# Transposing two heads at once, and putting the transposes behind the scores

## The chip, the cores and the metric

The kernel runs on one core of one Trainium2 chip. The metric is device time in microseconds of one execution, as the median over several. Times of single instructions come from one profiled execution, whose time differs a little from the median; both are given below.

## The reference

Eight batches, eight heads, 576 positions, head size 64. Causal attention with a decay bias, and behind it an MLP mixer: a token part (a product over positions) and a channel part (512 to 1536 to 512).

```python
scores = scale * np.matmul(q, k.transpose(0, 1, 3, 2))
s_pos = np.maximum(s, 0.0)
cum = np.cumsum(s_pos, axis=-1)
bias = -(cum[:, :, :, None] - cum[:, :, None, :])
scores = np.where(causal, -1000000000.0, scores + np.minimum(bias, 0.0))
attn = softmax(scores)
x = np.matmul(attn, v)                       # heads side by side: (8, 576, 512)
xt = x.transpose(0, 2, 1)
h = np.maximum(xt @ w_tok1, 0.0) @ w_tok2
u = x + h.transpose(0, 2, 1)
return u + np.maximum(u @ w_ch1, 0.0) @ w_ch2
```

(`softmax` stands for the subtraction of the maximum, the exponential and the division that the reference writes out.)

## The kernel before

All work is recorded as operations with the engines that may run them, an estimated duration on each, a priority and the tiles that they read and write. A planner (`Plan.run`) then goes through time, gives each free engine the ready operation of best priority, and hands out buffers from rings; the order that it finds is what is issued. TensorE (PE) runs matrix products, ScalarE (ACT) and VectorE (DVE) evict its results from PSUM and do the pointwise work, GpSimd (POOL) and the sync engine (SP) issue transfers. The planner's estimate of a change between 64-row and 128-row work on TensorE is the constant `SWITCH`; an operation with `mode=1` is 64-row work. A dependency given as `after` lets the second operation start as soon as the first has been issued.

Two rings lie in PSUM: `psc`, two buffers of two banks each (1024 float32), and `pmx`, four buffers of one bank. The channel part's products (L1039 for the first matrix, L1064 for the second), the token part's (L921, L983) and a few others use `pmx`; scores (L750) and the weighted sum of v (L821) use `psc`.

The work around the change goes by quads of four heads, two quads to a batch:

- `stage_qk` loads k and q of a quad in bfloat16 (L479). A tile `qkn` holds, for k and for q, two groups f of 9 x 64 numbers on each partition: partitions 0 to 63 are heads with e = 0, partitions 64 to 127 those with e = 1, and the nine blocks of 64 are positions p*9 + r. L664 takes sums of squares of `qkn` for a final check of ranges.
- `quad` transposes k (ti = 0) and then q (ti = 1). For each r, e and f one 64x64 transpose (L706) goes into PSUM, 36 for k and 36 for q. The data are the weights of the product and a 64x64 identity moves. Batch one writes into two `pmx` buffers, every later batch into the two banks of one `psc` buffer. Then ACT (L718) or DVE (L720) copies each half into `kT` or `qT`, in the right order of positions.
- `pair` takes two heads (f = 0 and 1 of one e), which lie in the two 64-row halves of the array. The scores stand in two pieces, each with a `psc` buffer and an operation of its own on TensorE: four products in the first and six in the second (L750). ACT takes the exponential (L758), DVE applies the causal mask (L767, L775), TensorE multiplies by v (L821, 18 products), and DVE divides (L850, L854).

The first quad of batch one comes by another way: it is loaded in float32 and cast by L541 and L543 into the same layout.

After attention, `tok` and `chan` do the mixer of a batch, whose products fill TensorE while the attention of the next batch goes on. Early gaps of TensorE are filled with products of zeros (L1160).

Of the kernel before, what the change touches and what calls it, by code (L numbers as in the profile page):

```python
# [9 lines left out]
BF16 = mybir.dt.bfloat16  # L10
# [22 lines left out]
class Buf:  # L33
# [14 lines left out]
    @property  # L48
    def t(self):
        return self.ring.tiles[self.slot]  # L50
# [187 lines left out]
def c_pe(n, f32=False):  # L238
    occ = n * (4 if f32 else 1) / 2400.0 + 0.0025
    return occ, occ + 0.21  # L240


def c_act(n, bias=False):
    occ = 0.08 + n * 0.00088 + (0.093 if bias else 0.0)
    return occ, occ + 0.1


def c_dve(n, two=False):
    occ = 0.1 + n * (0.00056 if two else 0.00104)
    return occ, occ + 0.12  # L250
# [121 lines left out]
def kernel(  # L372
# [12 lines left out]
    nc = tc.nc  # L385

    B, H, S, D = q.shape
# [7 lines left out]
    NQ = 512  # L395
    LAG = 2.5
    WARM = 45.0
    TOK = 2.0
    R = 9
    PR = S // R  # L400
# [9 lines left out]
    def ring(name, n, shape, dt, pool=None):  # L410
        p = pool or fast
        return Ring(name, [p.tile(shape, dt, name=f"{name}{i}", tag=f"{name}{i}") for i in range(n)])

    ident = sb("ident", [128, 128], BF16)
# [15 lines left out]
        return EB[jc] + (64 if odd else 128) if jc == NJ - 2 else EB[jc] - (64 if odd else 0)  # L430

    r_qn = ring("qkn", 5, [128, 2, 2, R * D], BF16)
    r_qT = ring("qT", 4, [128, S], BF16)
    r_kT = ring("kT", 4, [128, 640], BF16)
    r_E = ring("E", 4, [128, 2, EW], BF16)
# [13 lines left out]
    r_sc = ring("psc", 2, [128, 1024], FP32, psum)  # L449
    r_mx = ring("pmx", 4, [128, 512], FP32, psum)  # L450

    P = Plan()
# [52 lines left out]
    for i in range(2, 4):  # L505
        P.op({"DVE": (0.3, 0.5, lambda i=i: pads(nc.vector, i)), "POOL": (0.4, 0.6, lambda i=i: pads(nc.gpsimd, i))},
             writes=[("pad", i)], prio=40)
    P.op({"DVE": (0.6, 0.8, lambda: pads2(nc.vector)), "POOL": (1.0, 1.2, lambda: pads2(nc.gpsimd))},
         writes=["padw"], prio=41)
    P.op({"DVE": (0.3, 0.5, lambda: pads3(nc.vector, 1)), "POOL": (0.5, 0.7, lambda: pads3(nc.gpsimd, 1))},  # L510
         writes=["padv"], prio=42)
# [18 lines left out]
    first = Buf(r_qn)  # L530
    stage = r_gb.tiles[0][:, :, :].rearrange("p c n -> p (c n)").bitcast(FP32)
    stage = stage[:, 0 : 4 * R * D].rearrange("p (t f n) -> p t f n", t=2, f=2)
    for ti, src in enumerate((k, q)):
        def load0(ti=ti, src=src):
            nc.sync.dma_start(out=stage[:, ti, :, :],
                              in_=src[0, 0:4, :, :].rearrange("(f e) (p r) d -> (e p) f (r d)", e=2, r=R))
        P.op({"SP": (0.6, 4.0 + 0.9 * ti, load0)}, writes=[("stage", ti)], prio=-9 + ti)
        for f in range(2):
            def cast0(eng, ti=ti, f=f):
                if eng:  # L540
                    nc.vector.tensor_copy(out=first.t[:, ti, f, :], in_=stage[:, ti, f, :])  # L541
                else:
                    nc.scalar.copy(out=first.t[:, ti, f, :], in_=stage[:, ti, f, :])  # L543
            P.op({"ACT": (*c_act(576), lambda cast0=cast0: cast0(0)),
                  "DVE": (0.1 + 576 * 0.00104, 0.25 + 576 * 0.00104, lambda cast0=cast0: cast0(1))},
                 reads=[("stage", ti)], writes=[(first, ti, f)], prio=-6)
    P.op({"SP": (0.6, 4.8, lambda: nc.sync.dma_start(out=s_sb[:, :], in_=s.rearrange("b h s -> (b h) s")))},
         writes=["s"], prio=-7)
# [137 lines left out]
    xbuf = {}  # L686
    bd = Buf(r_mx, False)

    def quad(b, h):
        nat = qkn[(b, h)]  # L690
        np_ = (b * H + h) / 2
        dsts = [(Buf(r_kT), Buf(r_qT)) for e in range(2)]
        pads = [("pad", 2), ("pad", 3)] if b == 0 and h == 4 else []
        for ti in range(2):
            pts = [Buf(r_mx, False) for e in range(2)] if b == 0 else [Buf(r_sc, False)] * 2

            def pv(e, pts=pts):
                o = pts[e].t[:, :].bitcast(BF16)
                return o[:, 0:1024] if b == 0 else o[:, e * 1024 : e * 1024 + 1024]

            def tr(ti=ti, pv=pv):
                for r in range(R):
                    for e in range(2):
                        p0 = e * PR
                        for f in range(2):
                            nc.tensor.transpose(out=pv(e)[f * D : f * D + D, r * PR : (r + 1) * PR],  # L706
                                                in_=nat.t[p0 : p0 + PR, ti, f, r * D : (r + 1) * D],
                                                identity=ident[p0 : p0 + PR, p0 : p0 + PR])
            turn = P.op({"PE": (R * 0.031, R * 0.031 + 0.21, tr)}, reads=([(nat, ti, 0), (nat, ti, 1)] if b == 0 and h == 0 else [(nat, ti)]) + ["ident"] + pads,
                 writes=[(pts[e], e) for e in range(2)] + (["turned"] if b == 0 and h == 0 and ti == 0 else []), holds=[d[ti] for d in dsts], prio=(np_ - 30 * (b < 1 and h < 1), 2), mode=1)  # L710
            if b == 0 and h == 0 and ti == 1:
                scan.deps.add(turn)
            for e in range(2):
                def ev(eng, ti=ti, e=e, pv=pv):
                    i = pv(e)[:, 0:S].rearrange("d (r p) -> d p r", r=R)
                    o = dsts[e][ti].t[:, 0:S].rearrange("d (p r) -> d p r", r=R)
                    if eng == 0:
                        nc.scalar.copy(out=o, in_=i)  # L718
                    else:
                        nc.vector.tensor_copy(out=o, in_=i)  # L720
                P.op({"ACT": (*c_act(576), lambda ev=ev: ev(0)), "DVE": (*c_dve(576), lambda ev=ev: ev(1))},
                     reads=[(pts[e], e)], writes=[(dsts[e][ti], 0)], prio=1, alone=pts[e])
        for e in range(2):
            pair(b, h + e, *dsts[e])

    def pair(b, h, kT, qT):
        np_ = (b * H + h // 4 * 4) / 2 + h % 2
        E = Buf(r_E)
        odd = b % 2
        for pc, piece in enumerate(PIECES):  # L730
            ps = Buf(r_sc, False)
            c0 = 0
            cols = []
            for (jc, a, e) in piece:
                cols.append((jc, a, e, c0))
                c0 += e - a

            if b == 0:
                def preset(ps=ps, pc=pc):
                    for hh in range(2):  # L740
                        nc.tensor.matmul(out=ps.t[:, hh * 512 : hh * 512 + 512], lhsT=ident[:, :], rhs=neg[:, pc, :],  # L741
                                         start=True, stop=False)
                P.op({"PE": (2 * c_pe(512)[0], 2 * c_pe(512)[0] + 0.21, preset)}, reads=["neg", "ident"] + ["turned"],
                     writes=[(ps, 0)], prio=(np_ - 9, 0))

            def mm(ps=ps, cols=cols):
                for (jc, a, e, c0) in cols:
                    j0 = S - 128 if odd and jc == NJ - 1 else jc * 128
                    for hh in range(2):
                        nc.tensor.matmul(out=ps.t[:, hh * 512 + c0 : hh * 512 + c0 + e - a],  # L750
                                         lhsT=kT.t[hh * 64 : hh * 64 + 64, j0 : j0 + 128],
                                         rhs=qT.t[hh * 64 : hh * 64 + 64, a:e], start=b > 0, stop=b > 0 or jc == cols[-1][0])
            occ = sum(c_pe(e - a)[0] for (_, a, e, _) in cols)
            P.op({"PE": (occ, occ + 0.21, mm)}, reads=[(kT, 0), (qT, 0)], writes=[(ps, 0)], holds=[E], prio=(np_ - 9 * (b < 1), 1),
                 mode=1)

            def ex(ps=ps, pc=pc):
                nc.scalar.activation(out=E.t[:, :, 512 * pc : 512 * pc + 512],  # L758
                                     in_=ps.t[:, :].rearrange("p (e n) -> p e n", e=2), func=AF.Exp, scale=0.125)
            P.op(act(1024, ex), reads=[(ps, 0)], writes=[(E, jc) for (jc, a, e) in piece], prio=0)  # L760

            if b == 0:
                continue

            def mk(pc=pc):
                o = E.t[:, :, 512 * pc : 512 * pc + 512].rearrange("p e (c n) -> p e c n", c=2)[:, :, :, 0:128]
                nc.vector.tensor_tensor(  # L767
                    out=o, in0=o, in1=keep[:, :].unsqueeze(1).unsqueeze(1).to_broadcast([128, 2, 2, 128]), op=ALU.mult)
            P.op(dve(512, mk, True), reads=[(E, piece[0][0]), (E, piece[1][0]), "keep"],
                 writes=[(E, piece[0][0]), (E, piece[1][0])], prio=0, lock=True)  # L770
            if pc == 1:
                def mk4():
                    k0 = 64 if odd else 0
                    o = E.t[:, :, EB[4] : EB[4] + 64]
                    nc.vector.tensor_tensor(  # L775
                        out=o, in0=o, in1=keep[:, k0 : k0 + 64].unsqueeze(1).to_broadcast([128, 2, 64]), op=ALU.mult)
                P.op(dve(128, mk4, True), reads=[(E, 4), "keep"], writes=[(E, 4)], prio=0, lock=True)
# [431 lines left out]
```

## Time and profile before

| | us |
|---|---|
| median of three runs | 301.88 |
| lowest and highest | 301.61, 303.4 |
| the profiled execution | 302.87 |
| its span | 301.1 |

The granted clock of TensorE was 0.997 of full speed on average. The groups of the profile that the change touches, by line, engine and operation, with their count, busy time and mean duration of one instruction:

| group | count | busy us | mean ns |
|---|---|---|---|
| L706 PE, 64x64 transposes | 1152 | 14.0 | 195 |
| L750 PE, scores | 320 | 32.8 | |
| L718 ACT, evictions of transposes | 40 | 24.2 | 642 and 644 |
| L720 DVE, evictions of transposes | 24 | 17.5 | 753 and 754 |
| L758 ACT, exponentials | 64 | 62.2 | 1022 |

How to read it: products on TensorE are pipelined, so one transpose is recorded with 195 ns although 36 of them take 0.41 us. What a stretch of TensorE's stream costs is therefore read from the chain of waits in order of time, whose pieces do not overlap.

### The profile page before, as it was taken

Reading aid. Unit: us, or ns where it says so; the run is one execution under the profiler, and the core shown is the slowest. Engines: PE = TensorE matmul, PEld = TensorE weight load, DVE = VectorE, ACT = ScalarE, POOL = GpSimd, SP = SyncE. Lnnn points to the kernel's source line nnn. Section 1 sums busy time; section 2 is a strip of 40 time slices with the busy share of each in tenths; the row PEclk is TensorE's granted clock in tenths of the full one; section 3 lists DMA queues with packets and bytes.
Section 4 is the critical chain, followed back from the end, with each engine's and each line's share of the span. In section 5 each row is a group of like instructions: output and inputs, shape, how many; then the busy total and the mean of one; then the engine's idle time right before and its main releaser. Section 6 shows DMA issues by size and latency. Waiting matters only on the chain.

```text
span 301.1 us, 8152 instructions
## 1 busy us (share of the span) xinstructions
PE 292.5 (97%) x3432; PEld 168.0 (56%) x3432; DVE 187.5 (62%) x408; ACT 183.9 (61%) x300; POOL 80.6 (27%) x138
## 2 busy tenths in 40 slices
PE   8999999999999999999999999999999999999991
PEld 3478567576755455556754545447755444457550
DVE  5971889899987569756766548746868451520030
ACT  5778884779877678538792377128975275028300
POOL 8645678786630521007000000024100000000000
PEclk9999999999999999999999999999999999999998
DMA  7999989999999696258705200159635310250032
GB/s 213 227 206 207 210 191 235 189 241 229 203 235 162 154 227 108 65 137 194 121 2 105 108 35 2 54 140 184 106 67 101 110 37 0 71 159 0 4 112 68
DMA packets 38347, 39.28 MB, mean 130 GB/s; under 512 B 17600, under 2 KB 30976, under 8 KB 38304
## 3 DMA queue, kind: packets, MB, share of 16 engines
q0 software_dynamic: 17072, 24.25, 44.5%
q1 hardware_dynamic: 21232, 14.44, 18.5%
q8 instruction: 28, 0.46, 0.6%
q14 instruction: 15, 0.12, 0.1%
HBM read 40.65 MB, written 9.44 MB: 166 GB/s over the span
## 4 chain that ended last, share of the span: by engine, by line
PE 95%; DVE 1%; ACT 1%; issue 0%; DVEq 0%
PE pmx L1039 32%; PE pmx L1064 31%; PE psc L750 6%; PE pmx L983 6%; PE pmx L921 6%; PE psc L821 5%; PE psc L706 3%; PE pmx L1160 2%; PE psc L741 1%; ACT x L843 1%; PE pmx L706 1%; PE pmx L959 1%; DVE qT L720 0%; PE pmx L1008 0%; PE pmx L949 0%; DVE x L837 0%
## 5 line engine op out<-in xcount | busy, mean ns | idle before, releaser
L758 ACT ACTIVATE E<-psc 128x1024 bf16<-128x1024 f32 x64 | 62.2, 1022 | 29.0 <-PE psc L750 28.5
L1039 PEld LDWEIGHTS <-wc 128*128 128x128 bf16 x624 | 58.0, 98 | 31.2 <-issue 1.1
L1039 PE MATMUL pmx<-uTb,wc 128*128 128x320 bf16 (+2 forms) x384 | 55.6, 299 | 0.0
L1064 PE MATMUL pmx<-wc,gb 128*128 128x512 bf16 (+1 forms) x252 | 54.7, 369 | 0.0
L1039 PE MATMUL pmx<-uTa,wc 128*128 128x512 bf16 (+1 forms) x240 | 45.6, 337 | 0.0
L1064 PE MATMUL pmx<-wc,ga 128*128 128x512 bf16 x192 | 44.6, 379 | 0.0
L664 ACT ACTIVATE junk<-qkn 128x1152 bf16<-128x1152 bf16 x32 | 37.3, 1165 | 4.3 <-DMA qkn<-in_q_dram 3.9
L1064 PEld LDWEIGHTS <-gb 128*128 128x128 bf16 x252 | 23.7, 98 | 25.1
L1046 ACT ACTIVATE gb<-pmx 128x320 bf16<-128x320 f32 (+2 forms) x53 | 23.0, 436 | 20.0 <-PE pmx L1039 16.1
L630 POOL DMA_DIRECT2D vf<-in_v_dram x39 | 33.4, 870 | 4.6 <-issue 2.0
L767 DVE TENSOR_TENSOR E<-E,keep 128x512 bf16<-128x512 bf16 x56 | 22.9, 416 | 10.9 <-ACT E L758 10.7
L1064 PEld LDWEIGHTS <-ga 128*128 128x128 bf16 x192 | 18.1, 98 | 20.2 <-issue 0.2
L1046 ACT ACTIVATE ga<-pmx 128x512 bf16<-128x512 f32 (+1 forms) x43 | 22.8, 535 | 10.3 <-PE pmx L1039 9.5
L648 DVE TENSOR_TENSOR vp<-vf,wT 128x512 bf16<-128x512 f32 (+1 forms) x39 | 25.5, 686 | 1.5 <-DMA vf<-in_v_dram 1.3
L1048 DVE TENSOR_SCALAR gb<-pmx 128x320 bf16<-128x320 f32 (+2 forms) x43 | 20.9, 490 | 5.4 <-PE pmx L1039 4.3
L821 PEld LDWEIGHTS <-E 128*128 128x128 bf16 x576 | 21.1, 97 | 5.5
L718 ACT COPY kT<-psc 128x576 bf16<-128x576 bf16 x21 | 12.7, 642 | 18.4 <-PE psc L706 18.2
L854 DVE TENSOR_TENSOR x<-psc,rc 128x640 bf16<-128x640 f32 x28 | 23.0, 823 | 0.9
L1072 DVE TENSOR_TENSOR of<-pmx,ua 128x512 f32<-128x512 f32 x16 | 11.0, 688 | 18.0 <-PE pmx L1064 15.4
L479 POOL DMA_DIRECT2D qkn<-in_k_dram x19 | 13.8, 728 | 30.7 <-PE psc L706 14.5
L750 PE MATMUL psc<-qT,kT 64*128 64x256 bf16 (+2 forms) x320 | 21.8, 250 | 0.0
L479 POOL DMA_DIRECT2D qkn<-in_q_dram x19 | 13.7, 722 | 28.3 <-PE psc L706 25.4
(110 smaller groups left out, 300.0 us busy)
## 6 DMA issues: line engine op xcount, KB each, us to landing
vf<-in_v_dram POOLq DMA_DIRECT2D x32, 256.0 KB, 7.8
out_dram<-of SPq DMA_DIRECT2D x31, 256.0 KB, 2.2
qkn<-in_k_dram POOLq DMA_DIRECT2D x19, 288.0 KB, 7.1
qkn<-in_q_dram POOLq DMA_DIRECT2D x19, 288.0 KB, 7.6
wc<-in_moe_w_ch_dram POOLq DMA_DIRECT2D x8, 384.0 KB, 8.3
out_dram<-of SPq DMA_DIRECT2D x10, 128.0 KB, 2.3
vf<-in_v_dram POOLq DMA_DIRECT2D x7, 128.0 KB, 7.7
gb<-in_k_dram SPq DMA_DIRECT2D x1, 576.0 KB, 4.1
```

The costliest lines, as they stand in the source:

```text
L479: nc.gpsimd.dma_start(out=n.t[:, i, :, :], in_=src[b, h : h + 4, :, :].rearrange("(f e) (p r) d -> (e p) f (r d)", e=2, r=R))
L630: nc.gpsimd.dma_start(out=vf.t[p0 : p0 + n, c, :, :], in_=v[b, :, c * 128 : c * 128 + n, :].rearrange("h p d -> p h d"))
L648: eng.tensor_tensor(out=vp.t[p0 : p0 + n, c, :, 0:D], in0=vf.t[p0 : p0 + n, c, :, :], in1=wT[p0 : p0 + n, cw, b * H : b * H + H].unsqueeze ...
L664: nc.scalar.activation(out=junk[:, :].rearrange("p (t n) -> p t n", t=2), in_=i, func=AF.Square, accum_out=sq[:, col : col + 1])
L750: nc.tensor.matmul(out=ps.t[:, hh * 512 + c0 : hh * 512 + c0 + e - a], lhsT=kT.t[hh * 64 : hh * 64 + 64, j0 : j0 + 128], rhs=qT.t[hh * 64 ...
L758: nc.scalar.activation(out=E.t[:, :, 512 * pc : 512 * pc + 512], in_=ps.t[:, :].rearrange("p (e n) -> p e n", e=2), func=AF.Exp, scale=0.125)
L767: nc.vector.tensor_tensor(out=o, in0=o, in1=keep[:, :].unsqueeze(1).unsqueeze(1).to_broadcast([128, 2, 2, 128]), op=ALU.mult)
L821: nc.tensor.matmul(out=o[:, ic, 0:DE], lhsT=E.t[:, hh, d0 : d0 + 128], rhs=vp.t[:, jc, h + 2 * hh, 0:DE], start=(jc == j_lo), stop=(jc == ic))
L854: nc.vector.tensor_tensor(out=x.t[:, :, :].rearrange("p c (g f e d) -> p g e f c d", f=2, e=2, d=D)[:, h // 4, h % 2], in0=pav2()[:, :, :, ...
L1039: nc.tensor.matmul(out=pm.t[:, 0 : e - a], lhsT=wc1[:, m, cc * 128 : cc * 128 + 128], rhs=uT.t[:, m, a:e], start=(m == 0), stop=(m == NMC ...
L1046: lambda cc=cc, pm=pm, a=a, e=e: nc.scalar.activation(out=g.t[:, cc, a:e], in_=pm.t[:, 0 : e - a], func=AF.Relu),
L1064: nc.tensor.matmul(out=pm.t[:, na:ne], lhsT=g.t[:, cc, c * 128 : c * 128 + 128], rhs=wc2[:, cc, na:ne], start=(cc == 0), stop=(cc == NCC - 1))
```

## The change

Three things are changed.

- For batches two to eight a copy of 1152 elements on a partition, on ACT or DVE, puts the two groups f of k, and likewise of q, side by side (`qk`, a new ring of two). One block r is then 128 columns wide, and `tr_wide` makes one transpose of 64 rows by 128 columns where `tr` made two of 64x64. The first quad of batch one gets the same layout from its cast; its second quad keeps the old transposes.
- From batch three on (`JOIN`), the transposes of a quad go into two `pmx` buffers instead of a `psc` buffer, and those of k may start only once the first pair of the quad before has had its scores issued, those of q once its second pair has; their priority is raised.
- From batch two on (`BOTH`), the two pieces of a pair's scores are one operation of ten products that takes both `psc` buffers.

The planner's estimate of a transpose operation goes from 0.279 to 0.261 us.

```diff
+    JOIN = 4
+    BOTH = 2
...
+    r_qk = ring("qk", 2, [128, R, 2, D], BF16)
...
             def cast0(eng, ti=ti, f=f):
+                o = first.t[:, ti, :, :].rearrange("p f n -> p (f n)").rearrange("p (r f d) -> p r f d", r=R, f=2)[:, :, f, :]
+                i = stage[:, ti, f, :].rearrange("p (r d) -> p r d", r=R)
...
     def quad(b, h):
         nat = qkn[(b, h)]
+        gi = 2 * b + h // 4
+        join = gi >= JOIN
...
-            pts = [Buf(r_mx, False) for e in range(2)] if b == 0 else [Buf(r_sc, False)] * 2
+            apart = b == 0 or join
+            pts = [Buf(r_mx, False) for e in range(2)] if apart else [Buf(r_sc, False)] * 2
...
+            elif b:
+                qk = Buf(r_qk, False)
+
+                def turn_in(eng, ti=ti, qk=qk):
+                    o = qk.t[:, :, :, :].rearrange("p r f d -> p f r d")
+                    i = nat.t[:, ti, :, :].rearrange("p f (r d) -> p f r d", r=R)
+                    if eng:
+                        nc.vector.tensor_copy(out=o, in_=i)
+                    else:
+                        nc.scalar.copy(out=o, in_=i)
+                P.op({"ACT": (*c_act(1152), lambda t=turn_in: t(0)), "DVE": (*c_dve(1152, True), lambda t=turn_in: t(1))},
+                     reads=[(nat, ti)], writes=[(qk, 0)], prio=20, lock=True).late = 6
+                skey = [(qk, 0)]
...
+            wide = b > 0 or h == 0
+
+            def tr_wide(ti=ti, pv=pv, qk=qk if b else None):
+                t = (nat.t[:, ti, :, :].rearrange("p f n -> p (f n)").rearrange("p (r n) -> p r n", r=R) if b == 0 else
+                     qk.t[:, :, :, :].rearrange("p r f d -> p r (f d)"))
+                for r in range(R):
+                    for e in range(2):
+                        p0 = e * PR
+                        nc.tensor.transpose(out=pv(e)[:, r * PR : (r + 1) * PR], in_=t[p0 : p0 + PR, r, :],
+                                            identity=ident[p0 : p0 + PR, p0 : p0 + PR])
...
-            turn = P.op({"PE": (R * 0.031, R * 0.031 + 0.21, tr)}, reads=([(nat, ti, 0), (nat, ti, 1)] if b == 0 and h == 0 else [(nat, ti)]) + ["ident"] + pads,
-                 writes=[(pts[e], e) for e in range(2)] + (["turned"] if b == 0 and h == 0 and ti == 0 else []), holds=[d[ti] for d in dsts], prio=(np_ - 30 * (b < 1 and h < 1), 2), mode=1)
+            turn = P.op({"PE": (R * 0.029, R * 0.029 + 0.21, tr_wide if wide else tr)}, reads=skey + ["ident"] + pads,
+                 writes=[(pts[e], e) for e in range(2)] + (["turned"] if b == 0 and h == 0 and ti == 0 else []), holds=[d[ti] for d in dsts],
+                 prio=(np_ - 2 + ti, 2) if join else (np_ - 30 * (b < 1 and h < 1), 2), mode=1, after=scores[gi - 1, ti] if join else None)
...
     def pair(b, h, kT, qT):
...
+            pieces.append(ps)
+            todo.append((ps, sum(c_pe(e - a)[0] for (_, a, e, _) in cols), mm))
+            if both and pc == 0:
+                continue
+
+            def mms(todo=tuple(todo)):
+                for t in todo:
+                    t[2]()
+            occ = sum(t[1] for t in todo)
+            scores[gi, h % 2] = P.op(
+                {"PE": (occ, occ + 0.21, mms)}, reads=[(kT, 0), (qT, 0)], writes=[(t[0], 0) for t in todo], holds=[E],
+                prio=(np_ - 9 * (b < 1), 1), mode=1)
+            todo = []
```

More of the change, by code (lines that the diff above doesn't have):

```diff
@@ L539, in cast0 @@
             def cast0(eng, ti=ti, f=f):
+                o = first.t[:, ti, :, :].rearrange("p f n -> p (f n)").rearrange("p (r f d) -> p r f d", r=R, f=2)[:, :, f, :]
+                i = stage[:, ti, f, :].rearrange("p (r d) -> p r d", r=R)
                 if eng:
-                    nc.vector.tensor_copy(out=first.t[:, ti, f, :], in_=stage[:, ti, f, :])
+                    nc.vector.tensor_copy(out=o, in_=i)
                 else:
-                    nc.scalar.copy(out=first.t[:, ti, f, :], in_=stage[:, ti, f, :])
+                    nc.scalar.copy(out=o, in_=i)
             P.op({"ACT": (*c_act(576), lambda cast0=cast0: cast0(0)),
@@ L687 @@
     bd = Buf(r_mx, False)
+    scores = {}
     def quad(b, h):
         nat = qkn[(b, h)]
+        gi = 2 * b + h // 4
+        join = gi >= JOIN
         np_ = (b * H + h) / 2
@@ L694, in quad, with pv @@
         for ti in range(2):
-            pts = [Buf(r_mx, False) for e in range(2)] if b == 0 else [Buf(r_sc, False)] * 2
-            def pv(e, pts=pts):
+            apart = b == 0 or join
+            pts = [Buf(r_mx, False) for e in range(2)] if apart else [Buf(r_sc, False)] * 2
+            def pv(e, pts=pts, apart=apart):
                 o = pts[e].t[:, :].bitcast(BF16)
-                return o[:, 0:1024] if b == 0 else o[:, e * 1024 : e * 1024 + 1024]
+                return o[:, 0:1024] if apart else o[:, e * 1024 : e * 1024 + 1024]
+            if b == 0 and h == 0:
+                skey = [(nat, ti, 0), (nat, ti, 1)]
+            elif b:
[4 more added lines that the diff above has]
+                    if eng:
+                        nc.vector.tensor_copy(out=o, in_=i)
+                    else:
+                        nc.scalar.copy(out=o, in_=i)
+                P.op({"ACT": (*c_act(1152), lambda t=turn_in: t(0)), "DVE": (*c_dve(1152, True), lambda t=turn_in: t(1))},
+                     reads=[(nat, ti)], writes=[(qk, 0)], prio=20, lock=True).late = 6
+                skey = [(qk, 0)]
+            else:
+                skey = [(nat, ti)]
+            wide = b > 0 or h == 0
[7 more added lines that the diff above has]
+                                            identity=ident[p0 : p0 + PR, p0 : p0 + PR])
             def tr(ti=ti, pv=pv):
@@ L729, in pair @@
         odd = b % 2
+        gi = 2 * b + h // 4
+        both = gi >= BOTH
+        todo, pieces = [], []
         for pc, piece in enumerate(PIECES):
@@ L752, in mm @@
                                          rhs=qT.t[hh * 64 : hh * 64 + 64, a:e], start=b > 0, stop=b > 0 or jc == cols[-1][0])
-            occ = sum(c_pe(e - a)[0] for (_, a, e, _) in cols)
-            P.op({"PE": (occ, occ + 0.21, mm)}, reads=[(kT, 0), (qT, 0)], writes=[(ps, 0)], holds=[E], prio=(np_ - 9 * (b < 1), 1),
-                 mode=1)
+            pieces.append(ps)
[10 more added lines that the diff above has]
+            todo = []
+        for pc, piece in enumerate(PIECES):
+            ps = pieces[pc]
             def ex(ps=ps, pc=pc):
```

## The prediction

> **What bounds the kernel now.** I read the page's first part, then its chain of waits by engine and by line, then the table by stretches and TensorE's own waits.
>
> ```profile
> PE 292.5 (97%) x3432; PEld 168.0 (56%) x3432; DVE 187.5 (62%) x408; ACT 183.9 (61%) x300; POOL 80.6 (27%) x138
> ...
> PE 95%; DVE 1%; ACT 1%; issue 0%; DVEq 0%
> ...
> 66.00:115.00 49.00, 49.00 (x609) 28.25 (x612) 37.94 (x82) 37.70 (x59) 20.09 (x26) 1.00 1.07 196
> 115.00:165.00 50.00, 50.00 (x556) 28.17 (x557) 35.51 (x72) 32.74 (x52) 7.82 (x10) 1.00 0.51 103
> ```
>
> The last two rows are stretches: the columns are length, then PE, PEld, DVE, ACT and POOL busy, the granted clock (1.00 = full) and DMA. From 66 us on TensorE has no hole, and 95% of the chain is TensorE. Its waits name no other engine after the start:
>
> ```profile
> PE pmx L1160 <- DVE zero L487: 1.2, 1, 1.2
> PE pmx L803 <- DVE vp L659: 0.3, 1, 0.3
> PE pmx L921 <- issue: 0.2, 1, 0.2
> ```
>
> So time changes where TensorE's own stream gets shorter, or where DVE or ACT (37.9 and 37.7 of 49 us, 77%, in the first stretch) begin to make it wait. What its stream costs is best read from the chain in order of time, whose pieces do not overlap (start, length, what):
>
> ```profile
> 134.62 0.73 PE psc L706 x72
> ...
> 136.55 0.32 PE psc L750 x4
> 136.87 0.65 PE pmx L1039 x4
> 137.52 0.33 PE psc L750 x6
> 137.85 2.82 PE pmx L1039 x20
> 140.67 0.54 PE psc L821 x18
> ...
> 142.73 0.33 PE psc L750 x6
> 143.06 0.41 PE psc L706 x36
> 143.47 2.82 PE pmx L1039 x20
> 146.29 0.54 PE psc L821 x18
> 146.83 2.72 PE pmx L1039 x20
> 149.55 0.55 PE psc L750 x10
> ...
> 155.07 2.59 PE pmx L1064 x12
> ```
>
> Three prices stand in it. (a) **Leaving a 64-row burst**: the same twenty L1039 products take 2.82 us after a burst of L750 or L706 and 2.72 after L821, which uses all 128 rows: 0.10 us. (b) **Entering one**: scores in two bursts take 0.32 + 0.33, in one 0.55: 0.10 us. The L706 burst at 143.06 stands straight behind scores and still takes 0.41, so 64x64 tiles behind 64x128 tiles pay too: 36 more transposes within a burst cost 0.73 - 0.41 = 0.32, and 0.41 - 0.32 = 0.09 is the entry. (c) **The transposes themselves**: 0.32 us for 36, nine rounds of four quarter-array tiles, 36 ns a round.
>
> **Fewer changes of tile shape.** I counted runs of instructions of one tile shape along TensorE's order as built. Before: 125 changes of shape; 41 runs of scores, 23 of transposes (14 of 36, nine of 72), four of them adjacent to scores. After: 93; 20 runs of ten score products with 18 transposes behind, ten runs of 18 transposes alone, 15 of scores alone, two of 36 small transposes. That is 32 changes less, at 0.10 us each by (a) and (b): -3.2 us, provided that wide transposes count as the scores' shape. They are 64x128 like L750 (64 rows, 128 columns). If the switch to a transpose costs what any switch does, 20 of the joins give back 0.10 each, 2.0 us; that is one bound, zero the other. I take zero, since what told scores and L706 apart at 143.06 was the shape.
> The Trainium skill ("TensorEngine Tiling (Array Packing)", Key Properties) has it that changing the tiling mode drains TensorE while another tile of one mode does not; by that, too, the joins pay nothing. The 0.41 behind scores agrees for a change of column split; no row here has transposes and scores in one shape.
>
> **Wider transposes.** Thirty of 32 bursts of 36 become 18: nine rounds of two half-array tiles, each 64 rows by 128 columns of weights and 64 moving columns. Before does not contain them. Nearest rows:
>
> ```profile
> L821 PEld LDWEIGHTS <-E 128*128 128x128 bf16 x576 | 21.1, 97 | 5.5
> ...
> L750 PEld LDWEIGHTS <-kT 64*128 64x128 bf16 x320 | 12.5, 94 | 14.8 <-issue 12.1 <-ACT qT L718 0.5 <-ACT ga L1046 0.4
> ...
> L706 PEld LDWEIGHTS <-qkn 64*64 64x64 bf16 x1152 | 11.4, 107 | 7.2 <-issue 4.7 <-ACT qkn L543 1.3 <-DMA qkn<-in_k_dram 0.7
> ```
>
> L821 loads 128 columns and moves 65, and eighteen take 0.54 us, 30 ns each. If the two row halves run together, nine rounds of 30 ns are 0.27 us. If their loads go one after the other, it is eighteen times 30 ns, 0.54. If cost goes by instruction, as 0.32/36 = 9 ns, it is 0.16. I take 0.27: a 64x128 load is recorded at 94 ns, under the 107 of 64x64, so the wider load is not the slower one, and four L706 tiles share a 36 ns round, so loads of different tiles do overlap. Sum: before 32 x 0.32 = 10.2; after 30 x 0.27 + 2 x 0.32 = 8.7; -1.5 us. The bounds are -4.8 (0.16: 5.4 in all) and +6.6 (0.54: 16.8).
> The Trainium skill ("TensorE: Matmul & The Clock Gate", LDWEIGHTS) speaks against this part: it gives a load as its column count over 1.2, in ns, so 128 columns would be 107 ns and 64 half of that. By it nine rounds would be 0.96 us, and the change would lose some 17 us. The trace refutes that for this form of load, with 30 ns for a 128-column load and its product, so it gets no chance of its own.
>
> **The new copies and the moved evictions.** Twenty-eight copies of 1152 elements are added for batches two to eight, 18 on ACT, 10 on DVE in the built order, and evictions of the transposes go from 40 on ACT and 24 on DVE to 19 and 45.
>
> ```profile
> L664 ACT ACTIVATE junk<-qkn 128x1152 bf16<-128x1152 bf16 x32 | 37.3, 1165 | 4.3 <-DMA qkn<-in_q_dram 3.9
> ...
> L1046 ACT ACTIVATE gb<-pmx 128x320 bf16<-128x320 f32 x47 | 20.6, 437 | 18.5 <-PE pmx L1039 14.7
> ...
> L718 ACT COPY kT<-psc 128x576 bf16<-128x576 bf16 x21 | 12.7, 642 | 18.4 <-PE psc L706 18.2
> ...
> L1048 DVE TENSOR_SCALAR gb<-pmx 128x320 bf16<-128x320 f32 x25 | 12.2, 487 | 4.9 <-PE pmx L1039 4.3
> ...
> L720 DVE COPY kT<-psc 128x576 bf16<-128x576 bf16 x7 | 5.1, 753 | 0.5 <-ACT kT L718 0.4
> ...
> L565 DVE TENSOR_SCALAR neg<-keep 128x512 bf16<-128x512 bf16 x1 | 0.2, 222 | 0.0
> ```
>
> ACT: +18 x 1.165 - 21 x 0.642 = +7.5 us. DVE: +21 x 0.753 = 15.8, and ten copies of between 0.5 us (L565's 222 ns over 512 elements, 0.43 ns each) and 1.2 (ACT's price); by L565, which is the same engine and type, +5; together +21, to about 208 us, 69%. Neither becomes the bound on average, and a copy has the whole time from one burst of its kind to the next to finish in; behind it in its queue stand evictions, which TensorE meets through the four "pmx" banks. This is the new wait: from batch three on a burst takes two of these four until its evictions are done, while ACT does two exponentials. Walking one burst through the built order in a stretch of 320-column groups (0.54 us each; evicted in 0.44 or 0.49): DVE does one eviction of the transposes, a group, a mask, a group; the fifth group then waits some 0.1 us for its bank, and no other does. In 512-column groups and behind L1064, where one bank lasts up to 2.6 us, none waits. Eight of the 20 joined bursts stand ahead of 256- or 320-column groups. I put 1.0 us for all: 0.1 each, and as much again for copies that delay an eviction elsewhere. Bounds: nothing, or one whole eviction (0.75) at each of the eight, 6 us. A gain from the now freer "psc" banks I exclude: TensorE waits for none of them now.
>
> **The head.** The casts of the first quad write runs of 64 elements; their stage is the same. The second quad of batch two is the tight one:
>
> ```profile
> 26.71 0.73 POOL L479 DMA_DIRECT2D qkn<-in_k_dram  x1 [0.28 <-issue]
> ...
> 28.35 0.70 POOL L479 DMA_DIRECT2D qkn<-in_q_dram  x1 [0.27 <-issue]
> ...
> 35.55 0.48 PE L706 MATMUL psc<-ident,qkn 64*64 64x64 bf16 x36
> ...
> 36.94 0.48 PE L706 MATMUL psc<-ident,qkn 64*64 64x64 bf16 x36
> ...
> qkn<-in_q_dram POOLq DMA_DIRECT2D x19, 288.0 KB, 7.6
> ```
>
> q lands near 28.35 + 7.6 = 36.0, its transposes ran at 36.9, and a copy of 1.2 us now lies between. In the built order more L1039 groups stand ahead of the scores that need it, 16 instead of 12 products, so I cost it at nothing; without that cover it is 0.3 us.
>
> **Sum.** -3.2 - 1.5 + 1.0 = -3.7 us. The profiled execution took 302.87 us (span 301.1), 1.0 above the median of 301.88: 299.2 on its own footing, and 298.2 against the median.
>
> **Rivals.** *The banks eat it.* Each of the 20 joined bursts makes TensorE wait for a bank, not only some of them: at 0.2 us each, a quarter of an eviction, 4 us, so 301.9 - 4.7 + 4.0 = 301.2, no change. For it: 77% load in the stretch from 66 us, two banks less; against it: evictions are spread over two engines. *The loads go one after the other*, on the slower side: place, the 30 wide bursts; price, 0.54 for 0.32; 301.9 - 3.2 + 6.6 + 1.0 = 306.3. It decides from about 0.39 us a burst, where 30 bursts and the two small ones (30 x 0.39 + 0.64 = 12.4) cost 2.2 us more than the 10.2 before, which is what 3.2 - 1.0 leaves. For it: no row has 128-column loads of two row halves close together, since L750's hide behind 256 moving columns; against it: the 94 against 107 ns. *It doesn't do what it says*: a transpose behind scores still pays 0.10; then 300.2. *The instruction price*: 0.16 a burst, no waits: 301.9 - 3.2 - 4.8 = 293.9.
>
> **Chances.** Forecast 0.52, with a range of its own from 296.3 (0.24 us a burst and no waits: 301.9 - 3.2 - 2.4) to 299.7 (waits of 2.5 us); banks 0.18; joins that still pay 0.10; loads in series 0.08; 0.05 for a whole eviction waited for at twelve bursts, 301.9 - 4.7 + 9.0 = 306.2; instruction price 0.07. About 1% (3 us) is what a measurement of this kernel can tell from no change, so the bounds are 298.9 and 304.9. Faster by over 1%: two thirds of the forecast's 0.52, the 0.07, and 0.03 of the joins' case, 0.45. Slower by over 1%: the 0.08, the 0.05 and 0.04 from banks that cost more than I bound, 0.17. Within: 0.38. The range goes from 295.7 (0.22 us a burst, no waits: 301.9 - 3.2 - 3.0) to 303.2 (301.9 - 4.7 + 6.0) and leaves out the serial loads, the twelve waits and the instruction price, 0.20.
>
> **What would show it.** Chain pieces: a burst of ten scores and 18 transposes at 0.55 + 0.27, the group behind it 0.10 dearer; transposes alone 0.37. More than 0.5 for 18 means serial loads; 0.9 or more for the joined burst means that the join pays. Waits: rows of TensorE for L1046, L1048, L718 or L720 of over 3 us in sum mean the banks' rival. DVE near 208 us, ACT near 191. I am wrong altogether if TensorE's stretches from 66 us show holes, or if the sum of its stream is not 4 to 5 us shorter.

## The result and the profile after

The changed kernel takes 314.86 us (median of six runs, 313.72 to 317.7) against 302.41 for the kernel before on the same chip: 1.041 times the time, interval 1.036 to 1.046. It is slower, and the forecast of 298.2, with a range up to 303.2, was wrong in its sign. The profiled execution took 313.72 us, its span is 311.8. Medians, ratios and intervals leave out runs more than 1.5% above the fastest of the same kernel.

First the busy times, then the chain's shares by engine, both from the page of the changed kernel:

```profile
PE 287.4 (92%) x2860; PEld 169.0 (54%) x2893; DVE 205.8 (66%) x437; ACT 189.5 (61%) x298; POOL 83.2 (27%) x139
...
PE 76%; DMA 9%; DVE 8%; POOL 2%; issue 2%; ACT 1%; POOLq 0%; DVEq 0%
```

TensorE's recorded work is 5 us less than before (292.5), and the end still comes 10.7 us later. The 5 us are not an exact measure of the gain: 2860 products are on record for 2893 weight loads, so some records are missing, and some products ran slowly. But time was won in TensorE's stream, and more was lost in a place where it stands still. Its waits (who waited, for whom; total, times, longest) name that place:

```profile
PE pmx L1093 <- DMA uTa<-ua: 12.6, 1, 12.6
PE pmx L1214 <- DVE zero L490: 1.2, 1, 1.2
```

The first row is new. `uTa` holds the transposed activations of batch three's mixer, which SP's DMA transposes write (L1053); L1093 is the channel part's first product, L1039 before. The chain in order of time shows it with its surroundings, and further down what became of the transposes:

```profile
94.97 2.52 PE pmx L1118 x11
97.50 18.87 DMA uTa<-ua
116.37 0.14 issue
116.50 3.57 PE pmx L1093 x8
120.08 0.79 PE psc L875 x18
120.86 1.73 PE pmx L1093 x8
...
155.47 0.55 PE psc L792 x10
156.02 0.26 PE pmx L736 x18
156.28 3.37 PE pmx L1093 x24
```

Three losses stand here: the hole itself, 12.57 us up to 116.50; behind it the same eight products in 3.57 instead of 1.73, +1.84; and 18 products of L875 in 0.79 instead of 0.54, +0.25. The stretches of 4 us (PE busy, granted clock, DMA share, GB/s) tell why the products were slow:

```profile
106.00:110.00 4.00, 0.00 (x0) 0.61 0.98 104
110.00:114.00 4.00, 0.00 (x0) 0.50 1.22 115
114.00:118.00 4.00, 1.50 (x4) 0.50 1.12 244
118.00:122.00 4.00, 4.00 (x30) 0.69 0.88 208
122.00:126.00 4.00, 3.95 (x43) 1.00 0.01 3
```

The granted clock falls to 0.50 in the hole and returns some 4 us after the work does. In sum 12.57 + 1.84 + 0.25 = 14.66 us. Without them the span would be 297.1 against 301.1, 4.0 less, where the forecast had summed to 3.7 less. So nearly all of the miss is one thing that the forecast had no term for, at 14.7 us.

Why were the transposes late? In stretches from 88 to 104 us the table of DMA issues (count, KB, median us from issue to landing) has them, first before, then after:

```profile
uTa<-ua SPq DMA_TRANSPOSE x4, 5.0
```

```profile
uTa<-ua SPq DMA_TRANSPOSE x4, 16.2
```

SP starts to issue them at about the same time in both (90.63 and 91.69 us), and the activations are not late: VectorE has written `ua` by 92.35 us before and 93.41 after. But the four issues take 5.25 us before and 10.43 after, and the last one, issued at 97.50, lands 18.87 us later. What differs is what GpSimd had sent off. Its timeline before (start, length, what, and in brackets how long it had been idle and who ended that):

```profile
84.23 0.71 POOL L479 DMA_DIRECT2D qkn<-in_k_dram  x1 [0.52 <-ACT junk L664]
85.64 0.72 POOL L479 DMA_DIRECT2D qkn<-in_q_dram  x1 [0.70 <-DMA qkn<-in_k_dram]
100.89 0.71 POOL L479 DMA_DIRECT2D qkn<-in_k_dram  x1 [14.54 <-PE psc L706]
```

And after:

```profile
82.44 0.72 POOL L482 DMA_DIRECT2D qkn<-in_k_dram  x1 [6.46 <-ACT junk L669]
...
83.87 4.24 POOL L635 DMA_DIRECT2D vf<-in_v_dram  x5
88.09 0.73 POOL L482 DMA_DIRECT2D qkn<-in_k_dram  x1
88.80 0.75 POOL L482 DMA_DIRECT2D qkn<-in_q_dram  x1
90.75 0.72 POOL L482 DMA_DIRECT2D qkn<-in_k_dram  x1 [1.20 <-ACT junk L669]
91.46 0.72 POOL L482 DMA_DIRECT2D qkn<-in_q_dram  x1
```

Before, GpSimd stood for 14.54 us until the transposes L706 of an earlier quad had read the load buffer that the next load was to fill, and in that pause the loads already sent off ran out, so that SP's DMA transposes met few of them: from 94 to 96 us the queue of the loads moved 0.01 MB, and in the changed kernel 0.26. In the changed kernel the transposes read the copy `qk`. The load buffer is free once the copy and the squares (L669) are done, so in this stretch the next loads wait for L669 and not for TensorE, the pause is gone, and loads of 256 and 288 KB go out ahead of the transposes and among them.

The Trainium skill ("DMA: Bandwidth & Descriptors", Issuing engines are not separate DMA queues) says that DMAs started by different engines run on the same 16 DMA engines and interleave. The trace agrees: it is GpSimd's loads and SP's transposes that meet here, 5.0 us to landing without the crowd and 16.2 with it.

### The profile page after: what moved, and what is told of

Its sections match the earlier page's. It is cut to its first block, busy times and chain, and to the rows that moved or that the text cites. A ratio compares the mean times of both kernels' runs of the same rounds, so it can differ in the third digit from the quotient of the medians.

```text
span 311.8 us, 7100 instructions
## 1 busy us (share of the span) xinstructions
PE 287.4 (92%) x2860; PEld 169.0 (54%) x2893; DVE 205.8 (66%) x437; ACT 189.5 (61%) x298; POOL 83.2 (27%) x139
## 4 chain that ended last, share of the span: by engine, by line
PE 76%; DMA 9%; DVE 8%; POOL 2%; issue 2%; ACT 1%; POOLq 0%; DVEq 0%
PE pmx L1093 28%; PE pmx L1118 26%; DMA uTa<-ua 6%; PE pmx L975 5%; PE pmx L1037 5%; PE psc L875 4%; PE psc L792 4%; DMA w<-in_moe_w_tok_dram 3%; PE pmx L736 2%; DVE vp L653 2%; DVE pre L1177 1%; POOL vf L635 1%; DVE qT L759 1%; DVE gb L1102 1%; DVE ub L1044 1%
## 5 line engine op out<-in xcount | busy, mean ns | idle before, releaser
L1093 PEld LDWEIGHTS <-wc 128*128 128x128 bf16 x624 | 58.7, 98 | 44.3 <-issue 14.9
L1093 PE MATMUL pmx<-uTa,wc 128*128 128x512 bf16 (+1 forms) x235 | 46.5, 344 | 12.8 <-DMA uTa<-ua 12.6
L1093 PE MATMUL pmx<-uTb,wc 128*128 128x320 bf16 (+2 forms) x384 | 55.7, 299 | 0.1
L1118 PE MATMUL pmx<-wc,ga 128*128 128x512 bf16 x186 | 43.8, 379 | 0.4
L1100 ACT ACTIVATE ga<-pmx 128x512 bf16<-128x512 f32 (+1 forms) x47 | 24.3, 525 | 27.4 <-PE pmx L1093 26.4
L669 ACT ACTIVATE junk<-qkn 128x1152 bf16<-128x1152 bf16 x32 | 37.3, 1165 | 0.5
L875 PEld LDWEIGHTS <-E 128*128 128x128 bf16 x576 | 21.7, 98 | 6.5 <-issue 2.0
L1126 DVE TENSOR_TENSOR of<-pmx,ua 128x512 f32<-128x512 f32 x16 | 11.0, 689 | 17.3 <-PE pmx L1118 16.2
L722 ACT COPY qk<-qkn 128x1152 bf16<-128x1152 bf16 x18 | 21.0, 1167 | 1.9 <-DMA qkn<-in_q_dram 1.1
L875 PE MATMUL psc<-vp,E 128*128 128x65 bf16 x522 | 20.9, 194 | 0.9 <-DVE vp L653 0.8
L1102 DVE TENSOR_SCALAR ga<-pmx 128x256 bf16<-128x256 f32 (+1 forms) x13 | 6.9, 543 | 22.5 <-PE pmx L1093 19.4
```

What stands on the lines that cost most here:

```text
L669: nc.scalar.activation(out=junk[:, :].rearrange("p (t n) -> p t n", t=2), in_=i, func=AF.Square, accum_out=sq[:, col : col + 1])
L875: nc.tensor.matmul(out=o[:, ic, 0:DE], lhsT=E.t[:, hh, d0 : d0 + 128], rhs=vp.t[:, jc, h + 2 * hh, 0:DE], start=(jc == j_lo), stop=(jc == ic))
L1093: nc.tensor.matmul(out=pm.t[:, 0 : e - a], lhsT=wc1[:, m, cc * 128 : cc * 128 + 128], rhs=uT.t[:, m, a:e], start=(m == 0), stop=(m == NMC ...
L1100: lambda cc=cc, pm=pm, a=a, e=e: nc.scalar.activation(out=g.t[:, cc, a:e], in_=pm.t[:, 0 : e - a], func=AF.Relu),
L1102: lambda cc=cc, pm=pm, a=a, e=e: nc.vector.tensor_scalar_max(out=g.t[:, cc, a:e], in0=pm.t[:, 0 : e - a], scalar1=0.0)),
L1118: nc.tensor.matmul(out=pm.t[:, na:ne], lhsT=g.t[:, cc, c * 128 : c * 128 + 128], rhs=wc2[:, cc, na:ne], start=(cc == 0), stop=(cc == NCC - 1))
```

## The experiments

The theory: the copy lets the loads go early, they delay batch three's DMA transposes, and TensorE waits for those. Rivals: the new order of bursts makes the hole; or early loads and copies cost time in other places too. Ratios are to runs of the kernel before on the same chip.

| kernel | us | ratio and interval |
|---|---|---|
| changed, loads held | 301.46 | 0.995 (0.991 to 0.999) |
| changed, four load buffers | 315.52 | 1.042 (1.037 to 1.046) |
| changed, nothing joined | 313.39 | 1.036 (1.030 to 1.041) |
| changed, no copies | 307.02 | 1.014 (1.009 to 1.019) |
| changed, batch three's transposes on TensorE | 300.40 | 0.992 (0.989 to 0.995) |
| changed, loads held, q's copy later | 301.08 | 0.995 (0.992 to 0.998) |
| changed, loads held, nothing joined | 304.15 | 1.005 (1.002 to 1.008) |
| changed, transposes on TensorE, q's copy later | 306.33 | 1.012 (1.008 to 1.016) |
| before, six load buffers | 314.51 | 1.035 (1.029 to 1.042) |
| before, transposes on TensorE | 304.27 | 1.005 (1.002 to 1.007) |
| before, six buffers, transposes on TensorE | 304.11 | 1.004 (1.001 to 1.007) |

**Hold the loads back.** From the second quad of batch three on, GpSimd copies one element of a quad's finished `qT` before it issues the load that will use that quad's buffer again, so that the load comes about where it came before. `first_load` has the first load of each quad, and quad `gi + 5` uses the buffer of quad `gi` again (dots stand for code that is not shown).

```diff
...
+        o = first_load.get(gi + 5)
+        if o is not None and gi >= HOLD:
+            def late():
+                nc.gpsimd.tensor_copy(out=seen[0:1, 2:3], in_=dsts[1][1].t[0:1, 0:1])
+            w = P.op({"POOL": (0.12, 0.2, late)}, reads=[(dsts[1][1], 0)], writes=[("seen", 100 + gi)], prio=-1, after=o.prev)
+            o.deps.discard(o.prev)
+            o.deps.add(w)
+            o.after = w
```

> The changed kernel, but a GpSimd copy of one element of the evicted q makes the load of a quad (from the eleventh on) wait until the transposes of the quad that held its buffer are evicted, as the loads did before the change. Theory (loads that the copy lets start early fill the DMA queues ahead of the DMA transposes of batch three): no wait of TensorE for uTa over 2 us, transposes land in 2.5 to 6 us, and what is left is the gain of TensorE's stream: 297.5 to 300 us. Rival (the joined bursts and the fuller ACT and DVE make the token part of batch three late): the wait of 12.6 us stays, 312 us or more.

301.46 us, above the theory's 297.5 to 300: the wait for `uTa` is gone, with 13 us of the time. GpSimd's timeline has a pause of 6.53 us again, ended by the eviction of `qT` that the hold waits for:

```profile
91.73 0.74 POOL L488 DMA_DIRECT2D qkn<-in_q_dram  x1
99.00 0.23 POOL L773 CAST seen<-qT 1x1 f32<-1x1 bf16 x1 [6.53 <-DVE qT L767]
```

The table of DMA issues (88 to 104 us) has the transposes landing soon again, 6.4 us after issue:

```profile
uTa<-ua SPq DMA_TRANSPOSE x4, 6.4
```

The gain falls some 3 us short of what the 4.0 would give (span 300.2 in place of 297.1). TensorE's waits have one of 2.1 us for an eviction of k (`PE pmx L991 <- ACT kT L765`), and from 56 to 59 us, behind it, the clock is 0.56. On ScalarE the copy of q of batch three's first quad waits for its load to land, with k's evictions queued behind it.

**Put that copy behind k's evictions.** The same kernel, one dependency more (`k_out` holds the evictions of k):

```diff
...
+                if gi == 4 and ti == 1:
+                    P.ops[-1].deps.update(k_out)
```

> The changed kernel with the hold on the loads, and for the quad of index 4 the copy of q put behind the evictions of k on ScalarE. Theory (what is left of the hold's shortfall is the 2.1 us wait of the products of batch two for kT, with the lower clock behind it): that wait is gone, the transposes of uTa still land within 8 us, and the time is 297 to 300 us. Rival (the copies cost elsewhere, by ACT and DVE busy time): the wait goes and the time stays at 301 to 302.5.

301.08 us, the rival's figure, and the same ratio as without the edit: the wait for `kT` went, and 1.0 us for another eviction behind the same late load came in its place (`PE pmx L995 <- ACT h L1007`), with 0.6 us more for `gb` (`PE pmx L1113 <- DVE gb L1122`). ScalarE's squares wait for that load too. In the profiled execution, whose span of 299.0 is 1.9 above the 297.1, these two waits make 1.6; over the runs as a whole, what keeps the held versions above the forecast was not found.

**Fewer load buffers.** If five buffers make the loads early, would four bring them back?

```diff
-    r_qn = ring("qkn", 5, [128, 2, 2, R * D], BF16)
+    r_qn = ring("qkn", 4, [128, 2, 2, R * D], BF16)
```

> The changed kernel with four load buffers for k and q in place of five, so that the load of a quad waits for the copy of a nearer quad. Theory: loads start some eight us later or more, the transposes of batch three find short queues, 298 to 302 us (a little may be lost where a load becomes late). Rival: 312 us or more, since nothing on TensorE, ACT or DVE is changed.

No: 315.52 us, and 15.1 us of waiting for `uTa`. GpSimd waited for squares until 83.46 us and then sent twelve loads by 94.34 us, once more ahead of the transposes at 92.71 and among them. The first of them went 1 us later than with five buffers (82.44), not eight. The number of buffers is not what decides, but when the loads go.

**More load buffers in the kernel before.** The reverse, with nothing of the change: six buffers in place of five. This ran on two occasions.

> The kernel before with six load buffers for k and q in place of five and nothing else. Theory: the load that waited for transposes at 100 us starts at about 86 to 90, ahead of the DMA transposes, which then land late, and TensorE waits for uTa by 5 to 12 us: 307 to 314 us, without any part of the change. Rival: no change, 301 to 303.

> The kernel before with six load buffers instead of five, once more with rounds, since two runs gave 309.9 and 315.0 us. Theory (loads let go early ahead of the DMA transposes make the hole): 308 to 315 us, with a wait for uTa of 4 us or more. Rival (the two runs were disturbed by something else): 302 to 304.

The first gave 309.88 and 314.99 us, the second a median of 314.51 (this one is in the table). The wait for `uTa` was 4.0 us in the profiled execution of the first, 309.88 us long and a little under what was expected, and 8.6 in that of the second, 314.51 us long: the size of the hole varies between executions. GpSimd's timeline in the second:

```profile
85.67 0.72 POOL L479 DMA_DIRECT2D qkn<-in_q_dram  x1 [0.69 <-PE pmx L921]
87.22 0.72 POOL L479 DMA_DIRECT2D qkn<-in_k_dram  x1 [0.83 <-DMA qkn<-in_q_dram]
88.43 0.72 POOL L479 DMA_DIRECT2D qkn<-in_q_dram  x1 [0.50 <-PE pmx L1064]
...
91.37 3.32 POOL L630 DMA_DIRECT2D vf<-in_v_dram  x4 [0.74 <-DVE ua L990]
```

The load after the one at 85.67, which had waited for L706 until 100.89 with five buffers, goes at 87.22 now, with five of v behind it. The chain of the same kernel:

```profile
97.11 16.48 DMA uTa<-ua
113.59 0.14 issue
113.72 1.86 PE pmx L1039 x4
```

With no copy, no wide transpose and no join, loads that go early by a spare buffer make a hole at the same place, of 8.6 us, and behind it four products take 1.86 us, where four take 0.86 or 0.97 elsewhere.

**Take the joins out of the changed kernel.** `JOIN = 99`, so the transposes stand alone and in `psc`.

> The changed kernel without the joined bursts (JOIN 99): copies and wide transposes stay, transposes go into the psc buffers as before. Theory: the copy frees the load buffers as early as in the changed kernel, so the wait for uTa stays in some size, 308 to 317 us. Rival (the bursts in pmx make it): the wait is gone, 299 to 303 us.

313.39 us from two runs, with 9.6 us of waiting for `uTa`. The joins don't make the hole.

**Take the copies out.** From batch two on the transposes are 64x64 again, straight out of the load buffer; joins and undivided scores stay.

> The changed kernel without the copies: from batch two on the transposes are 64 by 64 straight out of the load's buffer, still joined to the pair's scores. Theory (it is the copy that frees the load's buffer and so lets the loads start early): no wait for uTa above 3 us, and TensorE pays for 36 narrow transposes and their changes of tile shape: 301 to 305 us. Rival (the new order of the bursts, not the copy, makes the hole): the wait for uTa of 9 us or more stays and the time is 312 or more.

307.02 us, between the two expectations, from two runs. The wait for `uTa` is gone, as the theory has it, and GpSimd stands again until the transposes have read the load buffer:

```profile
96.11 0.71 POOL L482 DMA_DIRECT2D qkn<-in_q_dram  x1 [9.51 <-PE pmx L744]
```

The four transposes land 4.2 us after issue. In place of that wait stands one of 2.2 us for the next batch's DMA transposes, with half the clock behind it, as the chain shows:

```profile
116.54 0.41 PE pmx L744 x36
...
131.55 7.80 DMA uTb<-us
139.34 0.14 issue
139.48 4.55 PE pmx L1093 x20
```

Twenty products at 4.55 for 2.72 and the wait of 2.2 make 4.1 us; 307 - 4.1 is 302.9, within the theory's 301 to 305. The narrow transposes cost 0.41 behind scores, where wide ones cost 0.26.

**Move batch three's transposes to TensorE**, with the loads as early as they are:

```diff
-            if b >= 2:
+            if b >= 3:
                 def trd(dst=dst, di=di, tc_=tc_):
                     nc.sync.dma_start_transpose(out=uT.t[:, :, tc_ * 128 : tc_ * 128 + 128], in_=dst.t[:, di, :])
```

> The changed kernel with the transposes of batch three's activations on TensorE instead of the DMA queues; the loads are as early as in the changed kernel. Theory (the loss is the DMA transposes queued among early loads, and nothing else of the early loads matters): no wait for uTa in batch two's place, TensorE takes some 1 us of transposes more, time 297 to 302 us. Rival (early loads and the copies hurt in other ways too, for instance by landing late themselves): 305 us or more, with a wait of another name.

300.40 us, faster than both kernels and the lowest median of all (its interval overlaps those of the two held versions), and no wait for `uTa`. Two rows of the chain have the 16 transposes:

```profile
93.74 0.67 PE pmx L1062 x12
...
95.22 0.33 PE pmx L1062 x4
```

They take 1.0 us; 297.1, the span of the changed kernel less its hole, and 1.0 make 298.1, and the span measured is 298.5.

Is it this move that gains, or the change? The kernel before got the same move, with five load buffers and with six:

> The kernel before, with nothing but the transposes of batch three's activations moved from the DMA queues to TensorE. If the gain of the changed kernel with that same move (300.4 against 302.6 us) is the gain of the wide, joined transposes, then the move alone gains nothing here: no wait for uTa stands in the kernel before, TensorE takes about 1.2 us more, so 303 to 304.5 us. Rival (the move itself is what gains, by freeing the DMA queues): 300.5 to 302.

> The kernel before with six load buffers, and batch three's transposes on TensorE. Theory (early loads hurt only through those DMA transposes): as with five buffers and the same move, 303 to 305 us. Rival (early loads hurt by themselves, by occupying the DMA queues or memory): 307 us or more.

304.27 and 304.11 us. The move by itself costs 1.4 us (0.7 to 2.0 by the interval); and with it a sixth buffer costs nothing, where without it that buffer costs some 11 us. So the early loads of six buffers hurt only through the DMA transposes. It also gives the gain of the change on equal ground: 0.9918 / 1.0045 = 0.987 (0.984 to 0.991, by the root of the two intervals' squares), 3.9 us less.

**What the joins bring**, with the loads held:

> The changed kernel with the hold, with no burst joined to a pair's scores. If a joined burst saves what the profile of the changed kernel shows (0.26 us against 0.37 us for 18, and a change of tile shape less), about 0.2 us for each of some 20 joins: 3 to 4 us over the hold's 301.5, so 304 to 306. If the joins are worth nothing (the rival that a joined burst still pays): 301 to 302.5.

304.15 us, by the ratios 3.0 more than with joins. The chain of this kernel has the transposes alone in 0.37 us for 18, or k's and q's together:

```profile
81.37 0.37 PE psc L744 x18
...
92.37 0.63 PE psc L744 x36
```

That is 0.11 more than behind scores, and 0.10 more for the group behind (twelve L1109 products take 1.74 there and 1.63 elsewhere). Twenty joins at 0.21 would be 4.2 us; where k's and q's go together, eight times in this chain, the two prices fall on the pair once, which leaves 2.5. The 3.0 measured lies between, but is not the price of joins alone: this kernel lacks the wait of 2.1 us for `kT`, and waits 1.9 us in place of 0.5 for a cast at its start. The two profiled executions have the same span, 300.2. So the prices of single bursts are shown, and the total only by the ratios.

**Both mends at once.** Transposes on TensorE and q's copy behind k's evictions:

> The changed kernel with batch three's transposes on TensorE and, for the quad of index 4, the copy of q behind the evictions of k on ScalarE. The first alone ran in 300.4 us, with one wait of 0.7 us for kT left at the start of batch two. Theory: that wait goes, 299 to 300.2 us. Rival (the wait only changes its name, as in the version with the hold, where a wait of 1.0 us for h stood in its place): 300 to 301.

306.33 us, 6 more than without the second edit; neither expectation had that. The waits have 2.5 us for `h` at batch three's start, 1.2 for `uTb` and 0.4 for `uTa`; between 40 and 60 us TensorE was busy 17.07 us instead of 19.10, at a clock of 0.91. One dependency more, and the planner's order changed far from it: the wait for `uTb` lies 87 us behind the one for `h`. Which of the moved instructions is to blame was not tried.

## Why the prediction was wrong

- **TensorE's stream: right in its prices.** A wide burst of 18 was put at 0.27 us and takes 0.26 behind scores; alone, at 0.37, and takes 0.37 (in the version without joins); a joined burst pays nothing to enter, and the group behind it 0.10 (24 products in 3.37 us, where twenty in 2.72 make 3.26). The sum of -3.7 stands against -4.0 in the changed kernel without its hole, and -3.9 where both kernels have the transposes on TensorE. That the sums come so near is in part luck: they hold 1.0 us for banks that did not come, and not the 1.2 us more that TensorE waits in the first 66 us for other things (0.5 for a cast of the first quad, which was costed at nothing, and 1.0 for v, 0.3 before). The rivals of serial loads, of joins that still pay, and of the instruction price fall by the same rows.
- **DVE and ACT: right.** 205.8 and 189.5 us, against 208 and 191; a copy takes 452 ns on DVE and 1153 on ACT (medians).
- **Waits for banks: too dear.** 1.0 us was put in, with an upper bound of 6 and a rival of 4. In the changed kernel TensorE waits for no eviction of transposes or of groups in `pmx`.
- **The copies: the step that failed.** The prediction costed "the new copies and the moved evictions" by engine time, by what stands behind a copy in its queue, and by banks. It did not follow the buffer that the copy reads. A copy that moves the last reader of a buffer to an earlier time also moves what refills it; here that is GpSimd's loads, and the sum had no term for GpSimd, SP or a transfer. That stood at nothing; the runs show 14.7 us in its place: 12.6 of waiting for the DMA transposes of `uTa`, and 2.1 of slow products behind it. The row that warned was in the trace of before: a load that had waited 14.54 us for L706, the operation that the change takes away from that buffer. Its wait looked free, as it was on no engine of the chain, and it was what kept further loads from going out ahead of the transposes.
- **The head.** No row of waits has the second quad of batch two, as forecast. Its kind of trouble, evictions behind a copy that waits for a load, came up a batch later, in the version with the loads held: 2.1 us and the clock behind it.
- **What would show it wrong** was named: holes in TensorE's stretches from 66 us. There is one, with its price of 14.7 us.

## What to carry to other kernels

When an edit takes a reader away from a buffer, ask what refills that buffer, when it will now start, and which transfer had its way clear because it started late. An idle time on an engine off the critical path can be the slack by which a critical transfer lands in time; cost the transfer at its landing in a crowd, not in the open. If an early transfer meets a critical one, move the critical one to another engine (1.0 us of TensorE here, for 14.7) or hold the early one, and test the edit's own gain with the collision gone.

## What the runs showed of the hardware

**DMA transposes and loads slow each other.** In stretches of 8 us (PE busy, clock, DMA share, GB/s) of the kernel before with six load buffers, first with DMA transposes, then with them on TensorE:

```profile
96.00:104.00 8.00, 7.79 (x114) 1.00 1.17 152
104.00:112.00 8.00, 0.64 (x10) 0.81 1.39 84
```

```profile
96.00:104.00 8.00, 7.95 (x60) 1.00 1.05 237
104.00:112.00 8.00, 7.95 (x61) 1.00 0.27 91
```

From 96 to 104 us the DMA engines are about as busy (1.17 against 1.05), and move 152 GB/s in place of 237; the four 256 KB loads of v issued between 88 and 104 us land after 14.0 us (median) with the transposes among them and after 9.1 without. The transposes land after 16.6 us there, and after 5.0 with five buffers. Whether the transposes take the engines' time or wait in them was not told apart.

**A hole of some 2 us can halve the clock.** TensorE's hole of 2.24 us in the kernel without copies was followed by a granted clock of 0.50 for 3 us:

```profile
137.00:140.00 3.00, 0.76 (x6) 0.99 0.94 265
140.00:143.00 3.00, 3.00 (x13) 0.50 1.09 318
143.00:146.00 3.00, 3.00 (x36) 0.94 0.38 65
```

The 2.24 us of waiting and the 1.83 of slow products behind it make 4.1. Holes of 2.08 us (loads held) and 2.48 (transposes on TensorE, q's copy later) also brought the clock to 0.50; holes of 1.97 us (four load buffers), 1.94 (loads held, nothing joined, at the start) and 1.0 (loads held, q's copy later) left it at 1.00. Two of them stand before the same products, first with the clock halved behind the hole, then without:

```profile
54.97 2.07 PE L991 MATMUL pmx<-x,w 128*128 128x256 bf16 x15 [2.08 <-ACT kT L765]
```

```profile
54.85 1.26 PE L975 MATMUL pmx<-x,w 128*128 128x256 bf16 x15 [1.97 <-ACT kT L757]
```

Whether the length decides, or the moment at which the hole falls, these few cases don't show. The Trainium skill ("TensorE: Matmul & The Clock Gate", What's actually happening) has the throttle come after an idle window of about 3.4 us; the holes of 2.08 to 2.48 us were shorter than that, and the measurement decides.
